# Attention of the first ten head pairs: k loaded on all 128 partitions, q with zero rows from memory, no clears on GpSimd

## The chip, the cores and the metric

The kernel runs on one core of a Trainium2 chip. The core has a matrix engine (TensorE, PE), a vector engine (VectorE, DVE), a scalar engine (ScalarE, ACT), a general engine (GpSimd, POOL) and an engine that only issues transfers (SyncE, SP); 16 DMA engines move the data. Each engine works through its own list of instructions in order and waits on semaphores. The metric is the device time of one execution in microseconds. A run of a kernel is compared with runs of the kernel before on the same chip.

## The reference

q, k and v have the shape (4, 12, 448, 64): batch, heads, sequence, head size. The attention is causal; its output x (4, 448, 768) goes through two mixing blocks, of which only the first touches the stage that is changed here.

```python
scores = scale * np.matmul(q, k.transpose(0, 1, 3, 2))
scores = np.where(mask, -1000000000.0, scores)
attn = np.exp(scores - max); attn = attn / (sum + 1e-09)
x = np.matmul(attn, v)
...
xt = x.transpose(0, 2, 1)
h = np.maximum(xt @ w_tok1, 0.0) @ w_tok2
u = x + h.transpose(0, 2, 1)
h2 = np.maximum(u @ w_ch1, 0.0) @ w_ch2
x = u + h2
...
theta = x @ w_theta; zr = x * cos(theta); zi = x * sin(theta)
y = einsum(w_tok_r, zr) + einsum(w_tok_i, zi)
u = x + y
out = u + np.maximum(u @ w_ch, 0.0)
```

All weights are 64-bit floats in memory.

## The kernel before, in words

The 48 heads are worked as 24 pairs of two heads, 7 steps to a pair (one for the 64-row tails of both heads, then three tiles of 128 rows for each head), 168 steps in all. A step computes scores on TensorE (L358), adds the mask and takes the maximum on VectorE (L367), the exponential on ScalarE (L369), and, 4 or 5 steps later, the product with v on TensorE (L407, L416, L424). Each step also has a share of other work: the 24 weight tiles of the channel mix are fetched as 64-bit words, rounded, split into two 16-bit parts and stored (`ROUNDINGS`; on ACT L177, on GpSimd L130 and L163, on VectorE L185, L186 and L197), and from step 53 on the channel-mix units run between the steps (`UNIT_STEPS`; L231 to L233).

q and k lie in memory as 64 rows (the head size) by 896 columns (two heads), and the host has written every row twice, so that 128 rows are there. `prep` (L276 to L305) brings them in, one pair ahead of its use. There are two kinds of pairs. The pairs 0 to 11 are native: scores are a 32-bit matmul over 128 partitions of which only 64 carry data. For these, 64 rows are loaded, and the other 64 partitions of both tiles are cleared (L281), on GpSimd but for pair 0, where VectorE does it. The pairs 12 to 23 are split: all 128 rows of q and k are loaded (`q_raw`, L288; `k_raw`, L290), ScalarE rounds them (L160) into `qs` and `kh`, and VectorE takes the remainders (L167).

Tiles come from pools by tag, and a tag has a number of buffers, here two each. A new tile of a tag takes the buffer of the tile two before it and must wait until that one's readers are done. Before, native q and split q and k have the tag `qk_raw`; native k and split `kh` have `kh`; split rounded q has `qs`.

The order on each engine is not the order of the code alone: a scheduler places the instructions by the priority of their block (`prep`, the scores and the products with v stand in blocks of high priority) and by when it believes that their inputs and buffers are free. Every instruction of an engine then runs in that fixed order. Transfers of q, k, v, weights and converted weights are all issued by SyncE; only q of pair 0 is issued by ScalarE.

Of the kernel before, what the change touches and what calls it, by code (L numbers as in the profile page):

```python
# [8 lines left out]
F32 = mybir.dt.float32  # L9
# [9 lines left out]
P = 128  # L19
B, H, S, D = 4, 12, 448, 64  # L20
E = H * D
NPR = H // 2
# [7 lines left out]
NATIVE = {0, 1, 2, 3, 4, 5, 6, 7, 8, 9, 10, 11}  # L30
# [2 lines left out]
KEEP, UBACK = 6, 16  # L33
ROUND_BITS, ROUND_FETCH, ROUND_SPLIT, ROUND_STORE = 1, 2, 3, 5
LATE_CONVERT = 16
FIRST_UNIT, DENSE, RATE = 53, 88, (42, 29)
UNIT_STEPS = [FIRST_UNIT + n * (DENSE - FIRST_UNIT) // 14 if n < 14 else
              DENSE + -(-(n - 14) * RATE[0] // RATE[1]) for n in range(72)]
# [16 lines left out]
def fused(ctx, tc, q, k, v, w_tok1, w_tok2, w_ch1, w_ch2, w_theta, w_tok, w_ch, out):  # L55
# [15 lines left out]
    nc = tc.nc  # L71
# [86 lines left out]
    def copy_to(eng, dst, src, scale=1.0):  # L158
        if eng == "A":
            nc.scalar.activation(dst, src, AF.Copy, scale=scale)  # L160
        else:
            e = nc.gpsimd if eng == "P" else nc.vector
            e.tensor_scalar(out=dst, in0=src, scalar1=scale, scalar2=0.0, op0=ALU.mult, op1=ALU.add)  # L163

    def rest_to(eng, dst, src, hi):
        e = nc.gpsimd if eng == "P" else nc.vector
        e.tensor_tensor(out=dst, in0=src, in1=f32v(hi) if hi.dtype == F32R else hi, op=ALU.subtract)  # L167
# [49 lines left out]
    def convert(src, kept, p):  # L217

        w, f = ws_tile(), wf_tile()
        load64(f, src, raw_tile())  # L220
        split_scaled("A", w, f, p, row_squares(f))
        nc.sync.dma_start(out=kept, in_=w)
# [14 lines left out]
    ap2 = att.enter_context(tc.tile_pool(name="ap2", bufs=2))  # L237
# [36 lines left out]
    loads = {}  # L274

    def prep(b, pr):  # L276
        qr = ap2.tile([P, 2 * S], F32, tag="qk_raw", name="q_raw", bufs=2)
        if b * NPR + pr in NATIVE:
            kr = ap2.tile([P, 2 * S], F32, tag="kh", name="k_pad")
            for t, src in ((kr, k), (qr, q)):  # L280
                (nc.vector if b * NPR + pr == 0 else nc.gpsimd).memset(t[64:128], 0.0)  # L281
                if b * NPR + pr == 0 and t is qr:
                    for c in (slice(0, 2 * P), slice(2 * P, 2 * S)):
                        nc.scalar.dma_start(out=t[0:64, c], in_=src[b, pr, 0:64, c])
                else:
                    loads[b * NPR + pr] = nc.sync.dma_start(out=t[0:64], in_=src[b, pr, 0:64])
        else:
            loads[b * NPR + pr] = nc.sync.dma_start(out=qr, in_=q[b, pr])  # L288
            kr = ap2.tile([P, 2 * S], F32, tag="qk_raw", name="k_raw", bufs=2)
            nc.sync.dma_start(out=kr, in_=k[b, pr])  # L290
        vr = ap2.tile([P, 9 * D], F32, tag="v_raw", name="v_raw")
        nc.sync.dma_start(out=vr, in_=v[b, pr])
        if b * NPR + pr in NATIVE:
            qs, kh, kl = qr, kr, None
        else:
            qs = ap2.tile([P, 2 * S], F32R, tag="qs", name="qs")
            copy_to(pick("qhi"), qs, qr)
            rest_to(pick("qlo"), qs[64:128], qr[64:128], qs[64:128])
            kh = ap2.tile([P, 2 * S], F32R, tag="kh", name="kh")
            copy_to(pick("khi"), kh, kr)  # L300
            kl = ap2.tile([P, 2 * S], F32R, tag="kl", name="kl")
            rest_to(pick("klo"), kl, kr, kh)
        if b * NPR + pr in NATPV:
            return qs, kh, kl, (vr,)
        return qs, kh, kl, (vr,)  # L305
# [280 lines left out]
    def convert_late(n):  # L586
        while made[0] < min(n, len(late)):
            with tc.issue_after(loads[min(LATE_CONVERT, max(loads))].ins):
                convert(*late[made[0]])
# [26 lines left out]
    def pick(what):  # L616
        turn[what] = turn.get(what, -1) + 1
        return eng[what][turn[what] % len(eng[what])]

    steps = [(b, pr, t) for b in range(B) for pr in range(NPR) for t in range(7)]  # L620
    parts = {(0, 0): prep(0, 0)}
    pairs, xgs, mixes = {}, {}, []

# [256 lines left out]
    for b in range(B):  # L880
# [43 lines left out]
        if b == 0:  # L924
# [11 lines left out]
            f = split_u2()  # L936
        else:
            n = 3 if b < B - 1 else 2
# [10 lines left out]
            f = split_u2()  # L949
# [5 lines left out]
def _lay(inputs):  # L955
    import numpy as np

    def c(a):
        a = np.ascontiguousarray(a)
        return a.view(np.uint64) if a.dtype == np.float64 else a  # L960

    rows = [slice(0, 64), slice(64, 192), slice(192, 320), slice(320, 448)]

    native = np.array([n in NATPV for n in range(B * NPR)]).reshape(B, NPR, 1, 1)

    def pairs(a, tails_first):
        t = a.reshape(B, NPR, 2, S, D).transpose(0, 1, 4, 2, 3)
        if tails_first:
            t = np.concatenate([t[..., 0, :64], t[..., 1, :64], t[..., 0, 64:], t[..., 1, 64:]], axis=3)
        else:  # L970
            back = np.concatenate([t[..., 0, r] for r in rows[::-1]] + [t[..., 1, :]], axis=3)
            t = np.where(native, t.reshape(B, NPR, D, 2 * S), back)
        t = t.reshape(B, NPR, D, 2 * S)
        return c(np.concatenate([t, t], axis=2))

    v = inputs["v"].reshape(B, NPR, 2, S, D)
    va, vb = v[:, :, 0], v[:, :, 1]
    blocks = []
    for r in rows[1:]:
        blocks += [va[:, :, r], vb[:, :, r]]  # L980
    a0, b0 = va[:, :, rows[0]], vb[:, :, rows[0]]
    zero = np.zeros_like(a0)
    for x, y in ((a0, np.where(native, a0, zero)), (np.where(native, b0, zero), b0), (a0, b0)):
        blocks.append(np.concatenate([x, y], axis=2))
    vl = np.concatenate(blocks, axis=3)
    t1 = inputs["moe_w_tok1"]
    t1 = np.concatenate([np.concatenate([t1[rows[0]], t1[rows[0]]], axis=0)] + [t1[r] for r in rows[1:]], axis=1)
    t2 = inputs["moe_w_tok2"].reshape(2, P, S).transpose(1, 0, 2).reshape(P, 2 * S)

    def lhs_tiles(w):  # L990
        n, m = w.shape
        return w.reshape(n // P, P, m // P, P).transpose(2, 1, 0, 3).reshape(m // P, P, n)

    ch2 = inputs["moe_w_ch2"]
    ch2 = np.concatenate([lhs_tiles(ch2[:FF // 2]), lhs_tiles(ch2[FF // 2:])], axis=0)
    wr, wi = inputs["moe2_w_tok_r"].T, inputs["moe2_w_tok_i"].T
    wk = np.stack([np.concatenate([wr[rows[0]], wi[rows[0]]], axis=0)] + [wr[r] for r in rows[1:]] + [wi[r] for r in rows[1:]])
    return {
        "q": pairs(inputs["q"], True), "k": pairs(inputs["k"], False), "v": c(vl),
        "w_tok1": c(t1), "w_tok2": c(t2),  # L1000
        "w_ch1": c(lhs_tiles(inputs["moe_w_ch1"])), "w_ch2": c(ch2),
        "w_theta": c(inputs["moe2_w_theta"].reshape(DT, P, E)), "w_tok": c(wk),
        "w_ch": c(lhs_tiles(inputs["moe2_w_ch"])),
    }
# [21 lines left out]
```

## Time and profile before

| | |
|---|---|
| time, median of 3 runs | 872.34 us (870.30 to 873.48) |
| profiled execution | 871.68 us, its span 869.9 us |
| TensorE busy | 839.3 us, 96% of the span |
| VectorE / ScalarE / GpSimd busy | 598.9 / 531.3 / 265.6 us |
| mean granted TensorE clock | 0.998 of full |

The page gives the busy time of an engine as the union of its instructions; ends of matmuls are modelled, so a busy TensorE is not one at its peak. The timeline's rows name a start, a length, the engine and line, the tiles written and read, how many instructions the row holds, and in brackets the idle time of the engine before them and what ended it. A row of an engine with a q (SPq) is its sequencer issuing a transfer.

### The profile page before, as it was taken

The numbers are of one execution on the slowest core, as the hardware profiler recorded it, in microseconds if no ns is written. First come the engines' busy times: TensorE is split into PE (matmuls) and PEld (weight loads), VectorE is DVE, ScalarE is ACT, GpSimd is POOL, SyncE is SP. The second block draws the span as 40 slices with busy tenths as digits, with TensorE's granted clock in tenths as the row PEclk, the third lists the DMA queues.
The fourth block names the chain that finished last, engine by engine and source line by source line (L and its number), as shares of the span: only waits on it lengthen the run. The fifth ranks groups of instructions, "written<-read, shape, count | busy, mean of one in ns | idle before, by whom it ended". The sixth has DMA issues, their size and how long they took to land.

```text
span 869.9 us, 16014 instructions
## 1 busy us (share of the span) xinstructions
PE 839.3 (96%) x5699; PEld 532.7 (61%) x5699; DVE 598.9 (69%) x1294; ACT 531.3 (61%) x1223; POOL 265.6 (31%) x445
## 2 busy tenths in 40 slices
PE   7999998899899999999999999999999999999997
PEld 6988856565657566576756655565555555555554
DVE  6788787999988556567774367669747548567541
ACT  6798786777767637367653276547647447456441
POOL 4366564547662220413222035331111001101000
PEclk9999999999999999999999999999999999999999
DMA  6866869999999976856475597702613123131012
GB/s 217 258 208 201 269 198 271 261 310 294 289 255 313 280 226 140 233 132 125 141 173 203 186 278 265 227 30 73 197 40 108 40 90 98 40 119 58 25 45 75
DMA packets 121024, 151.99 MB, mean 175 GB/s; under 512 B 76848, under 2 KB 88048, under 8 KB 120944
## 3 DMA queue, kind: packets, MB, share of 16 engines
q1 hardware_dynamic: 120400, 149.95, 59.4%
q0 software_dynamic: 384, 0.79, 0.4%
q8 instruction: 45, 0.74, 0.3%
q10 hardware_dynamic: 160, 0.23, 0.1%
q14 instruction: 35, 0.29, 0.1%
HBM read 110.56 MB, written 22.81 MB: 153 GB/s over the span
## 4 chain that ended last, share of the span: by engine, by line
PE 67%; DMA 10%; DVE 8%; ACT 5%; issue 5%; POOL 5%; SPq 0%; ACTq 0%; POOLq 0%; DVEq 0%
PE ps_mm L232 15%; PE ps_mm L231 15%; PE ps_mm L233 15%; DMA pt<-ph 5%; PE ps_sc L358 3%; PE ps_sc L231 3%; PE ps_sc L232 3%; PE ps_sc L233 3%; PE ps_pv L407 2%; DMA raw_w<-in_w_theta_dram 1%; PE ps_pv L424 1%; ACT junk L124 1%; ACT sb L369 1%; DVE sb L367 1%; PE ps_mm L376 1%
## 5 line engine op out<-in xcount | busy, mean ns | idle before, releaser
L231 PE MATMUL ps_mm<-h,ws 128*128 128x448 f16 x432 | 151.7, 354 | 1.6 <-DVE g L140 1.0
L232 PE MATMUL ps_mm<-h,ws 128*128 128x448 f16 x432 | 152.7, 354 | 0.1
L233 PE MATMUL ps_mm<-h,ws 128*128 128x448 f16 x432 | 152.5, 354 | 0.0
L231 PEld LDWEIGHTS <-ws 128*128 128x128 f16 x720 | 70.5, 98 | 67.2 <-issue 5.3
L233 PEld LDWEIGHTS <-ws 128*128 128x128 f16 x720 | 70.5, 98 | 63.9 <-issue 3.7
L232 PEld LDWEIGHTS <-ws 128*128 128x128 f16 x720 | 70.5, 98 | 62.5 <-issue 5.2
L369 ACT ACTIVATE sb<-sb,mx 128x320 f32<-128x320 f32 (+3 forms) x168 | 89.1, 533 | 25.6 <-DVE mx L367 25.0
L231 PE MATMUL ps_mm<-ut,ws 128*128 128x448 f16 x288 | 101.1, 353 | 1.4 <-DMA rawt<-x2d 1.3
L232 PE MATMUL ps_mm<-ut,ws 128*128 128x448 f16 x288 | 101.5, 353 | 0.8 <-DVE ut L197 0.8
L233 PE MATMUL ps_mm<-ut,ws 128*128 128x448 f16 x288 | 101.6, 353 | 0.0
L367 DVE CUSTOM_DVE_ANT_0 sb<-ps_sc,mask 128x320 f32<-128x320 f32 (+3 forms) x168 | 73.4, 455 | 17.7 <-PE ps_mm L376 11.3
L124 ACT ACTIVATE junk<-acc 128x448 bf16<-128x448 f32 x72 | 41.2, 572 | 59.1 <-DVE acc L912 41.3
L358 PE MATMUL ps_sc<-k_pad,q_raw 128*128 128x192 f32 (+3 forms) x168 | 56.9, 441 | 9.1 <-DMA k_pad<-in_k_dram 4.3
L787 POOL TENSOR_SCALAR tmp<-tmp 128x384 f32<-128x384 f32 x28 | 15.6, 556 | 148.6 <-ACT tmp L786 145.6
L388 DVE SCALAR_TENSOR_TENSOR ph<-sb,ph 128x128 f16<-128x128 f32 (+1 forms) x64 | 46.8, 736 | 19.0 <-ACT ph L160 18.3
L163 POOL TENSOR_SCALAR h<-t 128x448 f16<-128x448 f32 x48 | 35.2, 735 | 75.7 <-ACT t L497 75.2
L497 ACT ACTIVATE t<-ps_mm,c_scale 128x448 f32<-128x448 f32 x48 | 30.0, 625 | 41.3 <-PE ps_mm L233 36.2
L160 ACT ACTIVATE ph<-sb 128x128 f16<-128x128 f32 (+1 forms) x64 | 39.6, 625 | 25.6 <-DMA pt<-ph 25.3
L499 DVE TENSOR_TENSOR h<-t,h 128x448 f16<-128x448 f32 x48 | 32.0, 670 | 27.0 <-POOL h L163 26.9
L130 POOL TENSOR_SCALAR raw<-raw 128x768 f32<-128x768 f32 (+2 forms) x34 | 35.4, 1041 | 41.6 <-ACT wf L177 37.0
L231 PE MATMUL ps_sc<-th,ut 128*128 128x384 f16 x144 | 46.9, 326 | 0.0
L233 PE MATMUL ps_sc<-th,ut 128*128 128x384 f16 x144 | 46.8, 326 | 0.0
(218 smaller groups left out, 2119.4 us busy)
## 6 DMA issues: line engine op xcount, KB each, us to landing
ws<-w_c SPq DMA_DIRECT2D x120, 384.0 KB, 4.6
raw<-in_w_ch_dram SPq DMA_DIRECT2D x30, 768.0 KB, 5.6
w_c<-ws SPq DMA_DIRECT2D x30, 384.0 KB, 4.3
v_raw<-in_v_dram SPq DMA_DIRECT2D x24, 288.0 KB, 4.9
q_raw<-in_q_dram SPq DMA_DIRECT2D x12, 448.0 KB, 4.2
k_raw<-in_k_dram SPq DMA_DIRECT2D x12, 448.0 KB, 5.4
x2d<-acc SPq DMA_DIRECT2D x24, 224.0 KB, 3.8
acc<-x2d SPq DMA_DIRECT2D x24, 224.0 KB, 2.6
```

What stands on the lines that cost most here:

```text
L124: nc.scalar.activation(j[:, 0:src.shape[-1]], src, AF.Square, accum_out=dst)
L130: nc.gpsimd.tensor_scalar(out=dst, in0=a, scalar1=b, scalar2=c, op0=ALU.mult, op1=ALU.mult)
L160: nc.scalar.activation(dst, src, AF.Copy, scale=scale)
L163: e.tensor_scalar(out=dst, in0=src, scalar1=scale, scalar2=0.0, op0=ALU.mult, op1=ALU.add)
L231: nc.tensor.matmul(ps, lhsT=ka(a[:, 0]), rhs=kb(b[:, 0]), start=first, stop=False)
L232: nc.tensor.matmul(ps, lhsT=ka(a[:, 0]), rhs=kb(b[:, 1]), start=False, stop=False)
L233: return nc.tensor.matmul(ps, lhsT=ka(a[:, 1]), rhs=kb(b[:, 0]), start=False, stop=last)
L358: nc.tensor.matmul(ps[:, 0:n], lhsT=lhs, rhs=cut(pp.kh), start=True, stop=pp.kl is None)
L367: pp.first = nc.vector.tensor_tensor_reduce(out=sb, in0=src, in1=msk, op0=ALU.add, op1=ALU.min, scale=-0.125, scalar=3.0e38, accum_out=pp. ...
L369: pp.last = nc.scalar.activation(sb, sb, AF.Exp, bias=pp.mx[:, j:j + 1], scale=-1.0, accum_out=pp.sm[:, 2 + j:3 + j])
L388: nc.vector.scalar_tensor_tensor(out=lo, in0=both, scalar=PSC, in1=hi, op0=ALU.mult, op1=ALU.subtract)
L499: gates[0] = nc.vector.tensor_tensor(out=t[:, 1], in0=f, in1=t[:, 0], op=ALU.subtract)
```

## The change

Pairs 1 to 9 (`WHOLE` is 10; pair 0 keeps its own way) load all 128 rows of k and of q. The host now writes zeros into the lower 64 rows of q for the pairs 0 to 9, so that the product over 128 partitions is the same, and nothing is cleared for the pairs 1 to 9. The pairs 10 and 11 load and clear as before. Native q takes the tag `qs` (the rounded q of the split pairs) in place of `qk_raw`, which is left to the split pairs' raw q and k.

```diff
--- before.py
+++ after.py
@@ -33,6 +33,7 @@
 KEEP, UBACK = 6, 16
 ROUND_BITS, ROUND_FETCH, ROUND_SPLIT, ROUND_STORE = 1, 2, 3, 5
 LATE_CONVERT = 16
+WHOLE = 10
 FIRST_UNIT, DENSE, RATE = 53, 88, (42, 29)
 UNIT_STEPS = [FIRST_UNIT + n * (DENSE - FIRST_UNIT) // 14 if n < 14 else
               DENSE + -(-(n - 14) * RATE[0] // RATE[1]) for n in range(72)]
@@ -274,19 +275,26 @@
     loads = {}
 
     def prep(b, pr):
-        qr = ap2.tile([P, 2 * S], F32, tag="qk_raw", name="q_raw", bufs=2)
-        if b * NPR + pr in NATIVE:
+        n = b * NPR + pr
+        if n in NATIVE:
+            qr = ap2.tile([P, 2 * S], F32, tag="qs", name="q_raw")
             kr = ap2.tile([P, 2 * S], F32, tag="kh", name="k_pad")
-            for t, src in ((kr, k), (qr, q)):
-                (nc.vector if b * NPR + pr == 0 else nc.gpsimd).memset(t[64:128], 0.0)
-                if b * NPR + pr == 0 and t is qr:
-                    for c in (slice(0, 2 * P), slice(2 * P, 2 * S)):
-                        nc.scalar.dma_start(out=t[0:64, c], in_=src[b, pr, 0:64, c])
-                else:
-                    loads[b * NPR + pr] = nc.sync.dma_start(out=t[0:64], in_=src[b, pr, 0:64])
+            if n == 0:
+                nc.vector.memset(kr[64:128], 0.0)
+                loads[n] = nc.sync.dma_start(out=kr[0:64], in_=k[b, pr, 0:64])
+                nc.vector.memset(qr[64:128], 0.0)
+                for c in (slice(0, 2 * P), slice(2 * P, 2 * S)):
+                    nc.scalar.dma_start(out=qr[0:64, c], in_=q[b, pr, 0:64, c])
+            elif n < WHOLE:
+                nc.sync.dma_start(out=kr, in_=k[b, pr])
+                loads[n] = nc.sync.dma_start(out=qr, in_=q[b, pr])
+            else:
+                for t, src in ((kr, k), (qr, q)):
+                    nc.gpsimd.memset(t[64:128], 0.0)
+                    loads[n] = nc.sync.dma_start(out=t[0:64], in_=src[b, pr, 0:64])
         else:
-            loads[b * NPR + pr] = nc.sync.dma_start(out=qr, in_=q[b, pr])
-            kr = ap2.tile([P, 2 * S], F32, tag="qk_raw", name="k_raw", bufs=2)
+            qr, kr = (ap2.tile([P, 2 * S], F32, tag="qk_raw", name=f"{x}_raw", bufs=2) for x in "qk")
+            loads[n] = nc.sync.dma_start(out=qr, in_=q[b, pr])
             nc.sync.dma_start(out=kr, in_=k[b, pr])
         vr = ap2.tile([P, 9 * D], F32, tag="v_raw", name="v_raw")
         nc.sync.dma_start(out=vr, in_=v[b, pr])
@@ -971,7 +979,10 @@
             back = np.concatenate([t[..., 0, r] for r in rows[::-1]] + [t[..., 1, :]], axis=3)
             t = np.where(native, t.reshape(B, NPR, D, 2 * S), back)
         t = t.reshape(B, NPR, D, 2 * S)
-        return c(np.concatenate([t, t], axis=2))
+        if not tails_first:
+            return c(np.concatenate([t, t], axis=2))
+        whole = np.array([n < WHOLE for n in range(B * NPR)]).reshape(B, NPR, 1, 1)
+        return c(np.concatenate([t, np.where(whole, np.zeros_like(t), t)], axis=2))
 
     v = inputs["v"].reshape(B, NPR, 2, S, D)
     va, vb = v[:, :, 0], v[:, :, 1]
```

The scheduler makes another order of it. On SyncE at the program's start, before the change (`in_w_tok` are the token-mix weights, `in_w_ch` the channel-mix weights; the rows with 64x896 are native loads):

```order
L286 DMA k_pad<-in_k_dram 64x896 x2
L286 DMA q_raw<-in_q_dram 64x896
L292 DMA v_raw<-in_v_dram 128x576 x2
L173 DMA raw<-in_w_tok_dram 128x1024 x2
L173 DMA raw<-in_w_tok_dram 128x896
L286 DMA k_pad<-in_k_dram 64x896
L286 DMA q_raw<-in_q_dram 64x896
L173 DMA raw<-in_w_tok_dram 128x896
L173 DMA raw<-in_w_ch_dram 128x1536 x2
```

and with the change:

```order
L284 DMA k_pad<-in_k_dram 64x896
L289 DMA k_pad<-in_k_dram 128x896
L290 DMA q_raw<-in_q_dram 128x896
L300 DMA v_raw<-in_v_dram 128x576 x2
L174 DMA raw<-in_w_tok_dram 128x1024 x2
L174 DMA raw<-in_w_tok_dram 128x896
L297 DMA q_raw<-in_q_dram 128x896
L298 DMA k_raw<-in_k_dram 128x896
L289 DMA k_pad<-in_k_dram 128x896
L290 DMA q_raw<-in_q_dram 128x896
L174 DMA raw<-in_w_tok_dram 128x896
L174 DMA raw<-in_w_ch_dram 128x1536 x2
```

The two rows that are new ahead of pair 2's loads, `q_raw` of L297 and `k_raw` of L298, are those of pair 12, the first split pair; the 128x896 rows around them are the grown loads of pairs 1 and 2.

On ScalarE where pair 10 ends and pair 11 begins, before the change (`sm_2111` marks the exponentials of pair 10, `sm_2427` those of pair 11, `qs_2444` and `kh_2447` are pair 12's rounded q and k):

```order
L369 ACTIVATE sb_186,sm_2111<-sb_186,mx_2110 128x448 x2
L160 ACTIVATE ph_2416<-sb_186 128x896
L160 ACTIVATE xg0_2032<-x1_192 128x4x128
L160 ACTIVATE qs_2444<-q_raw_2438 128x896
L124 ACTIVATE junk_2196,sqb_2195<-wf_2170 128x768
L369 ACTIVATE sb_186,sm_2427<-sb_186,mx_2426 128x128
...
L160 ACTIVATE ph_2510<-sb_186 128x384
L160 ACTIVATE kh_2447<-k_raw_2440 128x896
L369 ACTIVATE sb_186,sm_2427<-sb_186,mx_2426 128x320
```

and with the change (`sm_2093` is pair 10, `sm_2409` pair 11, `qs_2426` and `kh_2429` are pair 12's rounded q and k, `qs_2693` and `kh_2696` pair 13's):

```order
L161 ACTIVATE ph_2239<-sb_186 128x640
L377 ACTIVATE sb_186,sm_2093<-sb_186,mx_2092 128x448
L161 ACTIVATE qs_2426<-q_raw_2420 128x896
L161 ACTIVATE kh_2429<-k_raw_2421 128x896
L505 ACTIVATE t_1886<-ps_mm_1867,c1_scale0_145 128x448
L161 ACTIVATE xg0_2014<-x1_192 128x4x128
L377 ACTIVATE sb_186,sm_2093<-sb_186,mx_2092 128x448
...
L161 ACTIVATE qs_2693<-q_raw_2687 128x896
L161 ACTIVATE kh_2696<-k_raw_2688 128x896
L161 ACTIVATE ph_2560<-sb_186 128x640
L377 ACTIVATE sb_186,sm_2409<-sb_186,mx_2408 128x448 x2
```

Pair 12's two roundings stood behind all of pair 10's exponentials, and that of k well inside pair 11; now both stand ahead of pair 10's last exponential, and pair 13's ahead of pair 11's last two.

On GpSimd at the start, before the change (L130 is a step of the rounding of weights, L429 a pair's sums):

```order
L257 MEMSET sb 128x64 x2
L281 MEMSET k_pad 64x896
L281 MEMSET q_raw 64x896
L241 AFFINE_SELECT mask<-mask 128x128
L130 TENSOR_SCALAR raw<-raw 128x512
L281 MEMSET k_pad 64x896
L281 MEMSET q_raw 64x896
L130 TENSOR_SCALAR raw<-raw 128x512
L429 TENSOR_SCALAR sm<-sm 128x7
L130 TENSOR_SCALAR sm<-own,sm 128x2
```

and with the change:

```order
L258 MEMSET sb 128x64 x2
L242 AFFINE_SELECT mask<-mask 128x128
L131 TENSOR_SCALAR raw<-raw 128x512 x2
L437 TENSOR_SCALAR sm<-sm 128x7
L131 TENSOR_SCALAR sm<-own,sm 128x2
```

The clears of L281 are gone, and the rest stands in the same order.

## Rows read from the trace of the kernel before

**Rows 1.** The page: busy us, share, instructions of each engine; shares of the chain.
```profile
PE 839.3 (96%) x5699; PEld 532.7 (61%) x5699; DVE 598.9 (69%) x1294; ACT 531.3 (61%) x1223; POOL 265.6 (31%) x445
...
PE 67%; DMA 10%; DVE 8%; ACT 5%; issue 5%; POOL 5%; SPq 0%; ACTq 0%; POOLq 0%; DVEq 0%
```

**Rows 2.** Windows: stretch, length, busy us by engine, PEclk, DMA share, GB/s.
```profile
12.00:125.00 113.00, 108.81 (x773) 92.02 (x772) 93.99 (x236) 93.67 (x257) 65.45 (x98) 1.00 0.70 222
125.00:275.00 150.00, 137.37 (x1102) 90.83 (x1101) 135.62 (x300) 105.88 (x253) 83.64 (x117) 0.99 1.04 281
275.00:869.00 594.00, 585.92 (x3809) 344.90 (x3807) 364.11 (x733) 326.66 (x702) 112.60 (x219) 1.00 0.47 138
```

**Rows 3.** Line 281 from 0 to 110 us: ns min/median/max, first and last; who waited.
```profile
L281 POOL MEMSET k_pad<- x9: 840/842/843, 2.3 to 105.4; 64x896 f32 x9
L281 POOL MEMSET q_raw<- x9: 838/841/848, 3.1 to 106.2; 64x896 f32 x9
...
  PEld ps_sc L358: 1.3, 1
```

**Rows 4.** VectorE's waits, 0 to 125 us: us in total, times, longest.
```profile
DVE ws L197 <- POOL ws L163: 5.5, 5, 1.8
DVE wf L185 <- POOL raw L130: 2.7, 6, 0.8
```

**Rows 5.** Timeline of SyncE: start, length, line, transfer, count.
```profile
12.80 0.54 SPq L286 DMA_DIRECT2D q_raw<-in_q_dram  x1
...
16.67 4.55 SPq L173 DMA_DIRECT2D raw<-in_w_ch_dram  x2
...
22.41 0.53 SPq L286 DMA_DIRECT2D q_raw<-in_q_dram  x1
...
162.21 0.90 SPq L288 DMA_DIRECT2D q_raw<-in_q_dram  x1
...
174.55 0.52 SPq L290 DMA_DIRECT2D k_raw<-in_k_dram  x1
```

**Rows 6.** Transfers issued from 12 to 20, then 20 to 30 us: KB, us to landing.
```profile
q_raw<-in_q_dram SPq DMA_DIRECT2D x1, 224.0 KB, 3.5
...
q_raw<-in_q_dram SPq DMA_DIRECT2D x1, 224.0 KB, 7.9
```

**Rows 7.** Timeline of TensorE: first scores of pairs 2, 3 and 11.
```profile
21.86 0.39 PE L358 MATMUL ps_sc<-k_pad,q_raw 128*128 128x128 f32 x2
...
32.02 0.47 PE L358 MATMUL ps_sc<-k_pad,q_raw 128*128 128x128 f32 x2
...
161.93 0.46 PE L358 MATMUL ps_sc<-k_pad,q_raw 128*128 128x128 f32 x2 [1.55 <-issue]
```

**Rows 8.** Windows near the start, with 64-row and with 128-row loads in flight.
```profile
4.00:6.00 2.00, 1.41 (x4) 0.93 (x4) 0.84 (x5) 0.49 (x2) 0.27 (x1) 1.00 1.05 206
8.00:10.00 2.00, 2.00 (x7) 1.39 (x6) 0.36 (x1) 0.52 (x3) 0.00 (x0) 1.00 1.02 404
```

**Rows 9.** Timeline of ScalarE: rounding of q and k, pairs 12 and 13.
```profile
167.30 0.95 ACT L160 ACTIVATE qs<-q_raw 128x896 fp32r<-128x896 f32 x1 [0.33 <-DMA q_raw<-in_q_dram]
...
178.57 0.95 ACT L160 ACTIVATE kh<-k_raw 128x896 fp32r<-128x896 f32 x1 [0.85 <-DMA k_raw<-in_k_dram]
...
185.02 0.96 ACT L160 ACTIVATE qs<-q_raw 128x896 fp32r<-128x896 f32 x1 [0.85 <-DMA q_raw<-in_q_dram]
...
189.08 0.95 ACT L160 ACTIVATE kh<-k_raw 128x896 fp32r<-128x896 f32 x1 [1.27 <-DMA k_raw<-in_k_dram]
```

**Rows 10.** Windows around pairs 11 and 12.
```profile
160.00:164.00 4.00, 1.41 (x19) 1.02 (x15) 4.00 (x10) 3.53 (x8) 1.72 (x3) 0.99 1.02 341
164.00:168.00 4.00, 4.00 (x15) 1.86 (x13) 4.00 (x11) 3.15 (x7) 1.18 (x3) 0.58 1.38 256
...
175.00:200.00 25.00, 24.32 (x209) 17.15 (x208) 22.78 (x54) 18.85 (x45) 11.08 (x18) 1.00 1.15 307
```

**Rows 11.** Waits of the whole execution: us in total, times, longest.
```profile
ACT kh L160 <- PE ps_sc L358: 5.5, 2, 3.1
```

## The prediction

> **What bounds the kernel now.** I read the page's busy line and chain first. TensorE is busy for 839.3 of 869.9 us and holds 67% of the chain that ended last; VectorE has 598.9 us, GpSimd only 265.6 [rows 1]. The windows by stage come next, because the change touches one stage [rows 2]. The reader is to see three numbers there. From 12 to 125 us (the pairs whose loads are changed) TensorE is busy 108.81 of 113 us, so it idles 4.2 us. From 125 to 275 us (the last native pairs and the first split ones) it idles 150 - 137.37 = 12.6 us, while VectorE works 135.62 of 150 and the DMA share is 1.04. After 275 us it idles 8.1 us in 594, and nothing there is changed. A gain can come only out of 4.2 + 12.6 us, and what TensorE loses there comes back nowhere, since the rest is packed.
>
> **The change part by part.** Times are summed against the profiled execution, 871.68 us, which is 1.8 us longer than its span of 869.9; the median of the three runs is 872.34, 0.7 higher.
>
> *The clears.* Pairs 1 to 9 lose two clears each: 9 at 842 ns and 9 at 841 ns, 15.1 us of GpSimd [rows 3]. GpSimd is busy 65.45 of the 113 us [rows 2], so it is not the bound. Who waits for it? TensorE's weight load once, 1.3 us, for a clear [rows 3]. VectorE waits 5.5 us for the split of converted weights and 2.7 us for the step before its rounding, 8.2 us in all [rows 4]. The clears are 15.1/65.45 = 23% of GpSimd's time there, so about 1.9 us of these waits would go. VectorE idles 19 us in that stretch, so little of that reaches TensorE. Bounds: 0, and -4.2 us (all of TensorE's idle time). I take -0.5, near the lower end of the effect, as TensorE's only wait for a clear was 1.3 us and lies beside earlier matmuls.
>
> *The doubled loads.* Each of the 18 loads grows by 229,376 bytes, 4.13 MB in all, 458,752 per pair. The share of the DMA engines is 0.70 in this stretch [rows 2], so there is room; what counts is whether a pair's rows land before its first score. Pair 3 is the tightest: its q was issued at 22.41 [rows 5], took 7.9 us [rows 6], landed at 30.3, and was first used at 32.02 [rows 7], a slack of 1.7 us. The window with 64-row loads in flight moved 206 GB/s at a share of 1.05, the one with 128-row loads 404 GB/s at 1.02 [rows 8]. Its extra 458,752 bytes cost 1.1 us at 404 and 2.2 us at 206, so between in time and 0.5 us late. I take 0, as the new loads have 128 rows, like those of the 404 row. [...]
>
> *Pair 12's loads.* Native q leaves the two `qk_raw` buffers, so pair 12's q and k find them free from the start. In the program's order they stand right behind the first three token-weight fetches, ahead of pair 2's loads; before, they stood far back, at 162.21 and 174.55 us [rows 5]. Two consequences. First, 917,504 bytes more lie ahead of pair 2, with 458,752 of pair 1's growth and 458,752 of its own: 1,835,008 bytes, 4.5 us at 404 GB/s and 8.9 at 206. Pair 2's q landed at 12.80 + 3.5 = 16.3 [rows 5, 6] and was first used at 21.86 [rows 7], a slack of 5.6 us: in time at one rate, 3.3 us late at the other. I take 0, the 404 row's side. Second, ScalarE's waits for these transfers go: 0.33 and 0.85 us for pair 12's q and k; pair 13's, which now can be issued earlier too, cost 0.85 and 1.27 [rows 9]. That is 3.3 us of ScalarE, but TensorE idles only 0.68 us between 175 and 200 [rows 10]. Bounds 0 and -0.7; I take -0.3.
>
> *The order around pairs 10 and 11.* The scheduler rebuilds it, with the same instructions. [...]
>
> Sum: -0.5 + 0 + 0 - 0.3 - 0.7 = -1.5; 871.7 - 1.5 = 870.2 us.
>
> **Rivals.**
>
> *A: the waits of 125 to 275 us shrink.* With pair 12's loads gone from the crowded stretch (DMA share 1.04) and the order there rebuilt, TensorE might lose half of its 12.6 us [rows 2]: 6.3 on top of -0.8 from the first and third terms (the stall from 160 to 168 is part of the 6.3): 871.7 - 0.8 - 6.3 = 864.6. For it speaks that TensorE's largest wait there sits exactly where the order changes; against it, that VectorE works 90% of this stretch and none of its work goes.
>
> *B: slower, ScalarE blocked by a buffer that it now shares.* Native q moves into the two `qs` buffers. Pair 12's rounded q therefore overwrites pair 10's q and must wait until TensorE has done pair 10's last score; before, its buffer was fresh. In the order this copy and k's now stand ahead of pair 10's last exponential, and pair 13's stand ahead of two of pair 11's. If TensorE is late with those scores, ScalarE stands still with exponentials, ReLUs and roundings behind it, VectorE's residues wait next, and then TensorE for their transposed output. The price by the nearest row is ScalarE's present wait of the same copy for such a score: 2 waits, 5.5 us [rows 11]. [...] It decides once the last score ends after ScalarE has come to the copy. Against it: now ScalarE reaches pair 12's q at 167.30 [rows 9], long after pair 10's scores ended and pair 11's began at 161.93 [rows 7].
>
> *C: the early pile-up.* All of the start's bytes move at the 206 row's rate, and pair 2's first score waits 3.3 us, as worked out above: 871.7 + 3.3 = 875.0. Its sign is a loss, but within what can be told. [...]
>
> **How the numbers follow.** A measurement of this kernel can tell about 0.5% from no change: 4.4 us, so faster means under 868.0 and slower over 876.7. My forecast, 870.2, gets 0.52; its bounds reach from 871.7 - 9.2 to 871.7 + 3.8 if all its terms go one way, of which I give 0.05 to under 868.0 and 0.02 to over 876.7. A gets 0.22, 0.20 of it under 868.0. B gets 0.14, 0.11 of it over 876.7. C gets 0.12, 0.02 of it over 876.7. So faster 0.25, slower 0.15, same 0.60. The range goes from 864, just under A's time, to 877; it leaves out most of B and the further half of A: about 2 in 10.
>
> **What would show it.** No clear is left on GpSimd before pair 10 and its busy time from 0 to 125 us falls by about 15 us, while TensorE's idle time from 12 to 125 us stays near 4 us: the first term is right. If it falls under 1 us, the clears cost more than I think. TensorE's row for pair 2's first score names no load as its releaser: C is wrong. The rate from 4 to 6 us rises above 300 GB/s: the doubled loads are free. ScalarE's rows for pair 12 show no wait for q or k: the third term. From 125 to 275 us TensorE's idle time tells the rest: about 12 us, forecast; 6 or less, A; over 16 with ScalarE waiting for a score ahead of `qs` or `kh`, B. Wrong altogether would be a difference that sits after 275 us.

## The result, and the profile after

The changed kernel takes 879.97 us (median of 6 runs, 875.38 to 882.38) against 871.93 us for the kernel before (6 runs): a ratio of 1.0091, with a 95% interval of 1.0069 to 1.0114. That is 8.0 us slower. The forecast was 870.2 us, its range 864 to 877.

The profiled execution took 882.38 us, the slowest of the six, with a span of 880.6, so it lies 10.7 us above the profiled one of before. A second profile of the same kernel, at 879.72 us (k4_change_again below), stands beside it where a reading rests on one execution. The page's busy line and chain of the changed kernel, against [rows 1]:

```profile
PE 845.5 (96%) x5699; PEld 537.6 (61%) x5699; DVE 597.4 (68%) x1294; ACT 531.0 (60%) x1223; POOL 254.3 (29%) x427
...
PE 70%; DVE 10%; DMA 8%; issue 4%; POOL 4%; ACT 3%; SPq 0%; ACTq 0%; DVEq 0%; POOLq 0%
```

TensorE runs the same 5699 instructions, but is busy 6.2 us longer (845.5 against 839.3), and is idle 35.1 us of the span in place of 30.6. Longer busy for the same work fits a lower clock (before, a 128x448 matmul of `h` and `ws` takes 0.35 us, and 0.58 us in the stretch of [rows 10]), and the windows show one. They stand here against [rows 2] and [rows 8] (length, then busy us of TensorE, its weight loads, VectorE, ScalarE and GpSimd, granted clock, DMA share, GB/s):

```profile
4.00:6.00 2.00, 0.96 (x4) 0.93 (x4) 0.16 (x1) 0.00 (x0) 0.00 (x0) 1.00 1.01 292
...
12.00:125.00 113.00, 107.83 (x760) 91.80 (x759) 93.09 (x235) 93.11 (x256) 51.86 (x81) 0.98 0.74 259
125.00:275.00 150.00, 139.11 (x1088) 91.44 (x1086) 136.75 (x304) 106.75 (x255) 89.24 (x116) 0.95 1.02 269
...
274.00:277.60 3.60, 1.18 (x4) 0.60 (x4) 2.91 (x9) 2.16 (x4) 2.92 (x4) 1.00 1.07 203
277.60:284.40 6.80, 4.12 (x19) 4.09 (x20) 1.53 (x3) 0.38 (x1) 1.16 (x1) 0.51 0.98 352
```

GpSimd lost its clears, 13.6 us of work in the second line. TensorE's idle time from 125 to 275 us even fell, from 12.6 to 10.9 us, but its granted clock there is 0.95 where it was 0.99. The last two lines show one case: TensorE works 1.18 of 3.6 us, and then runs at half clock (0.51 of full) for 6.8 us. There are five such stretches, beginning at 117, 155, 189, 216 and 278 us, 23.9 us in all; before there was one, 3.4 us [rows 10] (one more in the last microseconds of each is left out).

An engine at half clock counts as busy (before, 4.00 of 4 us at a granted 0.58 [rows 10]), so idle time does not show where the time went. I therefore compare progress. Each matmul counts with the time from its start to the next one's, for its kind in the trace of before (the 20th percentile); the sum is 815.8 us for every kernel here. The lag of a kernel at a time t is how much later than before it has done the work that before had done at t:

| lag in us at | 125 | 200 | 250 | 275 | 330 | 800 |
|---|---|---|---|---|---|---|
| changed kernel | 3.3 | 5.2 | 2.7 | 11.2 | 9.4 | 10.3 |
| changed kernel, second profile | 2.1 | 3.9 | 1.5 | 9.5 | 7.8 | 7.6 |

The lag swings by some us up to 250, grows by 8.5 and 8.0 us between 250 and 275, and stays. After 330 us it changes by less than 1 us.

The largest wait of TensorE at this step is not for a load of q or k. TensorE's row in the changed kernel (start, length, line, tiles, count, and in brackets the idle time and its releaser):

```profile
280.28 0.55 PE L232 MATMUL ps_mm<-h,ws 128*128 128x448 f16 x1 [4.31 <-DMA ws<-w_c]
```

SyncE's rows there, first of the changed kernel, then of the kernel before (start, time on SyncE, line, transfer, count):

```profile
267.48 0.33 SPq L589 DMA_DIRECT2D w_c<-ws  x1
268.07 0.32 SPq L528 DMA_DIRECT2D x2d<-acc  x1
268.81 7.31 SPq L399 DMA_TRANSPOSE pt<-ph  x2
276.21 0.53 SPq L227 DMA_DIRECT2D ws<-w_c  x1
```

```profile
260.24 0.32 SPq L581 DMA_DIRECT2D w_c<-ws  x1
...
265.07 1.81 SPq L226 DMA_DIRECT2D ws<-w_c  x4
266.98 6.82 SPq L391 DMA_TRANSPOSE pt<-ph  x2
```

These are the same transfers in another order. Before, four loads of converted weights `ws` stood ahead of two transposing DMAs, which hold SyncE for about 7 us; now they stand behind. The load also reads back what the store `w_c<-ws` ahead of it wrote, and that store now leaves 7.2 us later. None of these rows is in the diff: the scheduler has rebuilt the order.

### The profile page after: what moved, and what is told of

It is laid out like the page before. It is cut to its first block, busy times and chain, and to the rows that moved or that the text cites. A ratio compares the mean times of both kernels' runs of the same rounds, so it can differ in the third digit from the quotient of the medians.

```text
span 880.6 us, 15982 instructions
## 1 busy us (share of the span) xinstructions
PE 845.5 (96%) x5699; PEld 537.6 (61%) x5699; DVE 597.4 (68%) x1294; ACT 531.0 (60%) x1223; POOL 254.3 (29%) x427
## 4 chain that ended last, share of the span: by engine, by line
PE 70%; DVE 10%; DMA 8%; issue 4%; POOL 4%; ACT 3%; SPq 0%; ACTq 0%; DVEq 0%; POOLq 0%
PE ps_mm L233 16%; PE ps_mm L232 16%; PE ps_mm L234 16%; PE ps_sc L366 3%; PE ps_sc L232 3%; PE ps_sc L233 3%; PE ps_sc L234 3%; DMA pt<-ph 3%; PE ps_pv L415 2%; DMA ws<-w_c 2%; PE ps_pv L432 2%; DVE ph L396 1%; POOL raw L131 1%; DVE wf L186 1%; ACT sb L377 1%
## 5 line engine op out<-in xcount | busy, mean ns | idle before, releaser
L375 DVE CUSTOM_DVE_ANT_0 sb<-ps_sc,mask 128x320 f32<-128x320 f32 (+3 forms) x168 | 73.8, 454 | 25.3 <-PE ps_mm L384 10.2
L366 PE MATMUL ps_sc<-k_pad,q_raw 128*128 128x192 f32 (+3 forms) x168 | 59.3, 452 | 6.5 <-DMA q_raw<-in_q_dram 5.6
L164 POOL TENSOR_SCALAR h<-t 128x448 f16<-128x448 f32 x48 | 31.8, 664 | 108.4 <-ACT t L505 107.9
L131 POOL TENSOR_SCALAR raw<-raw 128x768 f32<-128x768 f32 (+2 forms) x34 | 37.4, 1101 | 36.5 <-ACT wf L178 36.1
```

Source lines behind the costliest of these rows:

```text
L131: nc.gpsimd.tensor_scalar(out=dst, in0=a, scalar1=b, scalar2=c, op0=ALU.mult, op1=ALU.mult)
L366: nc.tensor.matmul(ps[:, 0:n], lhsT=lhs, rhs=cut(pp.kh), start=True, stop=pp.kl is None)
L375: pp.first = nc.vector.tensor_tensor_reduce(out=sb, in0=src, in1=msk, op0=ALU.add, op1=ALU.min, scale=-0.125, scalar=3.0e38, accum_out=pp. ...
```

## The experiments

Ratios are to the kernel before, run on the same chip in the same job. Compare runs of different jobs by their ratios, not by their times: the kernel before took 871.17 to 871.93 us in the other jobs, but 869.82 in that of l1 and l2. "Held order" means that the instructions of an engine were bound to a written list by edges that order the issue and add no wait (f1 and f4 below, both held, are at 0.9993 and 0.9990 of the kernel before, which is not, so holding costs nothing that can be seen):

```diff
+ORDER = (
...
+def pin(tc, nc):
...
+        row = [by[e][n] for n in accumulate(steps)]
+        for a, b in zip(row, row[1:]):
+            tc.add_manual_dep(b, a.name, mybir.DependencyInfo(
+                mybir.DependencyClass.NoSync, mybir.DependencyReason.DATA), reason="order")
...
         fused(tc, *args)
+        pin(tc, nc)
```

### Parts of the change alone

e1_room: only the moved room of native q.

```diff
-WHOLE = 10
+WHOLE = 1
```

> The changed kernel with WHOLE = 1: native q lies in the split pairs' buffers, but pairs 1 to 9 load 64 rows again and GpSimd clears the other half. Theory 1 (the loss lies in the order that is rebuilt around 105 to 285 us once native q leaves qk_raw and pair 12's loads go to the start: short waits of TensorE, each followed by a stretch at half clock): about as slow as the changed kernel, 876 to 882 us, with 15 us or more at half clock against 3.4 us before. Theory 2 (the 4.1 MB of added bytes): as before, 870 to 873. Theory 3 (the missing clears or the whole loads alone change the order for the worse): as before, 870 to 873, one or two falls of the clock. Theory 4 (ScalarE held by the shared buffers): 876 to 882, with ScalarE's rounding of q or k waiting for a score of TensorE.

Measured: 884.19 us, 1.0132 (1.0107 to 1.0157).

e2_whole: only the whole loads and the missing clears.

```diff
-            qr = ap2.tile([P, 2 * S], F32, tag="qs", name="q_raw")
+            qr = ap2.tile([P, 2 * S], F32, tag="qk_raw", name="q_raw", bufs=2)
```

> The changed kernel with native q back in qk_raw (two buffers, shared with the split pairs' raw q and k): only the whole loads, the zero rows and the missing clears are left of the change. Theory 1 (order around pairs 10 to 12 from the moved room and the early loads): as before or a little faster, 868 to 872 us, half-clock time as before (3.4 us). Theory 2 (added bytes): 876 to 882 with waits for loads in the first 125 us. Theory 3 (missing clears or whole loads change the order for the worse): 876 to 882 with the falls of the clock of the changed kernel.

Measured: 878.78 us, 1.0080 (1.0055 to 1.0104).

e3_late12: the whole change, with pair 12's loads late as before.

```diff
                 if nx == (0, 1):
                     es.enter_context(tc.issue_after(loads[0].ins))
+                if nx == (2, 0):
+                    es.enter_context(tc.issue_after(loads[11].ins))
```

> The changed kernel with one more constraint: pair 12's loads are not issued before pair 11's (so they don't stand at the program's start); everything else is as changed. If pair 12's early loads are what rebuilds the order for the worse (a form of theory 1): back to 868 to 873 us with one or two falls of the clock. If it is the moved room as such, the bytes (theory 2) or the clears (theory 3): 876 to 882 and three or more falls of the clock.

Measured: 884.24 us, 1.0132 (1.0109 to 1.0155).

e4_dve11: a neutral edit of the kernel before.

```diff
-                (nc.vector if b * NPR + pr == 0 else nc.gpsimd).memset(t[64:128], 0.0)
+                (nc.vector if b * NPR + pr in (0, 11) else nc.gpsimd).memset(t[64:128], 0.0)
```

> The kernel before with one neutral edit: pair 11's two clears are put on VectorE instead of GpSimd (two more VectorE instructions under 1 us each, no load and no byte is changed), which makes the scheduler rebuild the order after it. If any rebuilt order costs waits and falls of the clock (the placebo view of theory 1): 874 to 882 us with 10 us or more at half clock. If the loss belongs to what this change moves: 871 to 873, at most 1 us for the two clears, one or two falls of the clock.

Measured: 880.78 us, 1.0097 (1.0077 to 1.0116).

All four are slower. Each half of the change costs about as much alone as the whole or more, so they don't add up; and moving two clears, with no load and no byte changed, costs the same 1%. Theory 1 in its first form, in which the moved room rebuilds the order for the worse, misses e2, and e3 refutes the early loads as the cause; e1 and e4 move no added byte, so theory 2 can't explain them. That any rebuilt order loses fits all four. Time at half clock does not follow the loss: 23.9 us in e1, 10.2 in e2, 17.1 in e3 and e4. TensorE's longest wait from 100 to 330 us is not the same in all, here in the order e1 to e4 (releaser: us in total, times, longest us):

```profile
PE ps_mm L232 <- DMA ws<-w_c: 6.6, 2, 5.7
```

```profile
PE ps_pv L432 <- DMA pt<-ph: 4.2, 2, 3.2
```

```profile
PE ps_sc L366 <- DVE mx L375: 7.8, 5, 2.8
```

```profile
PE ps_pv L424 <- DMA pt<-ph: 2.7, 2, 2.5
```

Weights, a transposed block, a score's bank, a transposed block: no one resource is short. Nor do they lose at one place: by the lag defined above, e2 is 6.7 us and e3 8.5 us behind at 250 us already, where the changed kernel is 2.7.

### The order held

f1_change_in_old_order has the whole change, and the held order of the kernel before:

> The whole change (whole loads, zero rows, no clears on GpSimd, native q in the split pairs' buffers), with the instructions of each engine held in the order of the kernel before: the same rows in the same places on TensorE, VectorE, ScalarE and SyncE, on GpSimd the same less the 18 clears; only sizes of loads and buffers differ. Order theory (the loss is what a rebuilt order does): 869 to 873 us, clock down once (3 to 4 us), within 2 us of before. Bytes or buffers (the added 4.1 MB, or the shared room, cost the time by themselves): 877 to 882 with the waits of the changed kernel. If the parts have a gain that the new order hides: under 868.

Measured: 871.04 us, 0.9993 (0.9978 to 1.0009), 12 runs. The time is as the order theory had it, the clock is not: it is down three times in the profile (10.2 us), not once.

f2_dve11_in_old_order has the neutral edit in the same held order:

> The neutral edit (pair 11's two clears on VectorE) with every engine held in the order of the kernel before, so that only the two clears have changed their engine. Order theory: 870 to 873 us. If the two clears on VectorE cost the 10 us themselves: 878 to 882.

Measured: 873.36 us, 1.0020 (1.0002 to 1.0038). Of the 0.97% of e4, the two clears by themselves thus account for some 0.2% (0.02 to 0.38).

f3_before_in_new_order has the kernel before in the order of e4_dve11:

> The kernel before, its clears on GpSimd and its loads unchanged, with TensorE, VectorE, ScalarE, SyncE and GpSimd held in the order that the neutral edit produced. Order theory: 878 to 883 us, as the neutral edit, with four or five falls of the clock. If the order is indifferent: 870 to 873.

Measured: 882.73 us, 1.0119 (1.0100 to 1.0137), with three falls of the clock (13.7 us), not four or five.

f4_early12 frees SyncE alone; it then loads pair 12 early:

> The whole change with TensorE, VectorE, ScalarE and GpSimd held in the order of the kernel before, and SyncE in an order of its own, in which pair 12's q and k are loaded near the program's start, ahead of pair 3's, and a few loads stand elsewhere. Order theory in its narrow form (what matters is the computing engines' order): 869 to 873 us. If the early loads cost by a pile-up at the start: 873 to 878, with TensorE waiting for q or k of pairs 2 to 4 in the first 60 us. If SyncE's order alone makes the late waits: above 875 with waits for transposed blocks or ws after 150 us.

Measured: 871.01 us, 0.9990 (0.9978 to 1.0003), 12 runs.

This is the decisive group. The same change costs 0.91% in the order that the scheduler makes of it and nothing in the old order; the unchanged kernel becomes 1.19% slower in a new order. The 4.1 MB more, the shared buffers, the early loads and the missing clears are all in f1 or f4, and all free there to within 0.2%. The windows of f1_change_in_old_order show what the change does by itself, but for pair 12's early loads, which are in f4 alone:

```profile
12.00:125.00 113.00, 109.55 (x781) 92.68 (x780) 96.34 (x240) 94.95 (x260) 55.69 (x84) 1.00 0.75 260
125.00:275.00 150.00, 137.41 (x1084) 92.31 (x1084) 134.20 (x296) 104.16 (x248) 82.35 (x115) 0.97 1.02 277
```

TensorE idles 3.45 us in the first stretch (4.2 before) and 12.6 in the second (12.6 before).

### Where the new order loses

g1_ws_ahead and g2_ws_behind exchange the rows on SyncE that were shown above, everything else held: g1 in the changed kernel's own order, g2 the other way round in the order of before.

```diff
+DMA ws<-w_c                x4   (g1; g2 the reverse)
 DMA_TRANSPOSE pt<-ph       x2
...
-DMA ws<-w_c                x4
```

> The changed kernel held in its own order on every engine, but for one place of SyncE's order: the four loads of ws that stand behind the two transposing DMAs of 268.81 us (7.31 us) now stand ahead of them, as in the kernel before. Order theory with single misplaced rows as the price: TensorE's wait of 4.31 us at 280 us goes, and the fall of the clock behind it (277.6 to 284.4 us) with it, so 873.5 to 876 us. If the time only moves to the next wait (the transposed blocks come 2 us later, or VectorE is the bound there): 878 to 881.

Measured: 879.07 us, 1.0084 (1.0061 to 1.0107). A miss: little came back.

> The reverse in the kernel before: held in its own order, but the four loads of ws that it issues at 265.07 us now stand behind the two transposing DMAs of 266.98 us (6.82 us). Order theory: the loads leave some 7 us later, TensorE waits for ws 5 to 7 us at about 269 us and the clock falls behind it: 876 to 881 us. If such a place is harmless, since TensorE's later work catches up: 871 to 874.

Measured: 880.31 us, 1.0097 (1.0071 to 1.0124). TensorE's row of g2_ws_behind:

```profile
278.33 0.56 PE L231 MATMUL ps_mm<-h,ws 128*128 128x448 f16 x1 [7.77 <-DMA ws<-w_c]
```

One exchange of rows on an engine that computes nothing costs the kernel before 8.8 us. In g1 the reverse gives little back, though TensorE's wait for `ws` does shrink, from 4.31 to 1.40 us (at 272.0 us). One reason is in the trace: the load that now stands ahead must wait 5.7 us for the store before it, and leaves 6.7 us after that store's issue. It is not the whole of it: g1's profile lags by 3.3 us at 330 us and by 6.4 at 800, 2.2 of these at a half-clock stretch near 640 us that the changed kernel's two profiles don't have. SyncE's waits, and its rows, in g1_ws_ahead:

```profile
SPq L227 <- DMA w_c<-ws: 5.7, 1, 5.7
```

```profile
262.07 0.43 SPq L589 DMA_DIRECT2D w_c<-ws  x1
262.67 0.32 SPq L528 DMA_DIRECT2D x2d<-acc  x1
268.77 1.74 SPq L227 DMA_DIRECT2D ws<-w_c  x4
270.62 6.51 SPq L399 DMA_TRANSPOSE pt<-ph  x2
```

k1_old_then_new and k2_new_then_old put two orders together at 245 us.

> The changed kernel, with every engine in the order of the kernel before up to what had begun by 245 us there, and the rest in the order of the changed kernel. If the new order loses after 245 us (TensorE's lag behind before at equal work grew from 2.7 to 11.2 us between 250 and 275 us in the changed kernel's trace): 877 to 881 us. If the loss lies in what the new order does before 245 us: 870 to 873. If it is spread over both: 873 to 877 here and in the run with the halves exchanged.

Measured: 880.04 us, 1.0101 (1.0083 to 1.0120).

> The halves exchanged: the order of the changed kernel up to what had begun by 245 us in its trace, and the rest in the order of the kernel before. If the new order loses after 245 us: 871 to 875 us. If it loses before: 877 to 881. If it is spread over both: 873 to 877.

Measured: 873.98 us, 1.0027 (1.0007 to 1.0048).

So the new order after 245 us loses about as much alone (1.0101) as the whole of it (1.0091, and 1.0103 in k4 below); before 245 us it costs some 2 us (1.0027, with an interval of 0.6 to 4.2 us). The windows of 245 to 285 us in the kernel before, the changed kernel, k1 and k2, one fence each in this order:

```profile
245.00:285.00 40.00, 37.64 (x309) 25.07 (x308) 35.95 (x77) 27.92 (x72) 14.22 (x20) 1.00 0.98 294
```

```profile
245.00:285.00 40.00, 32.74 (x222) 20.82 (x220) 33.28 (x69) 22.25 (x50) 21.05 (x25) 0.91 1.00 286
```

```profile
245.00:285.00 40.00, 33.18 (x208) 21.51 (x208) 31.49 (x66) 21.26 (x52) 17.04 (x20) 0.83 0.94 276
```

```profile
245.00:285.00 40.00, 37.37 (x311) 24.79 (x310) 34.55 (x76) 25.43 (x67) 15.65 (x21) 1.00 1.00 279
```

In 40 us the two with the new order there start 222 and 208 matmuls, the two with the old order 309 and 311.

k3_both takes the exchange of g1 into k1; k4_change_again runs the changed kernel once more.

> As k1_old_then_new (old order to 245 us, then the new), but with the four loads of ws ahead of the two transposing DMAs (7.27 us) behind which they stand in the new order, as in g1_ws_ahead. In k1_old_then_new TensorE waits 3.41 us for ws at 276.6 us, and runs at half clock from 274.8 to 281.6 us. If this place carries most of what the new order loses after 245 us: 873 to 876 us, 4 us or more under k1_old_then_new. If it is only one among several: 877 to 879.

Measured: 877.89 us, 1.0075 (1.0054 to 1.0097): one place among several, by the expectation, and its interval overlaps that of k1.

> The changed kernel unchanged, once more, so that g1_ws_ahead and k3_both can be compared with more than six runs of it: 879 to 881 us.

Measured: 879.58 us, 1.0103 (1.0079 to 1.0126). Its half-clock stretches begin at 116, 153, 188, 215 and 276 us: the same five places as in the first profile (mean granted clock 0.986, and 0.985 there).

In the changed kernel, what makes the store late is one row on VectorE. These weights are split in two steps: GpSimd writes the rounded part, VectorE the residue, and then the store goes. GpSimd's row and VectorE's rows of the changed kernel:

```profile
260.43 0.91 POOL L164 TENSOR_SCALAR ws<-wf,s 128x768 f16<-128x768 f32 x1
```

```profile
260.60 1.68 DVE L168 TENSOR_TENSOR kl<-k_raw,kh 128x896 fp32r<-128x896 f32 x1
262.20 0.94 DVE L187 SCALAR_TENSOR_TENSOR wf<-raw,wf 128x768 uint32<-128x768 uint32 x1
263.06 0.48 DVE L375 CUSTOM_DVE_ANT_0 sb<-ps_sc,mask 128x320 f32<-128x320 f32 x1
...
264.18 1.09 DVE L168 TENSOR_TENSOR qs<-q_raw,qs 64x896 fp32r<-64x896 f32 x1
...
266.45 1.01 DVE L198 SCALAR_TENSOR_TENSOR ws<-wf,s,ws 128x768 f16<-128x768 f32 x1
```

The same two in the kernel before:

```profile
258.25 0.91 POOL L163 TENSOR_SCALAR ws<-wf,s 128x768 f16<-128x768 f32 x1
```

```profile
259.19 1.02 DVE L197 SCALAR_TENSOR_TENSOR ws<-wf,s,ws 128x768 f16<-128x768 f32 x1
```

Before, the residue began 0.03 us after GpSimd was done; now it begins 5.1 us after, behind the rounding residues of pair 17's k and q, two scores and other rows. l1_chain (in the changed kernel's own order) and l2_chain (in k1) put the whole chain in place:

```diff
 on VectorE
 TENSOR_TENSOR kl<-k_raw,kh
+SCALAR_TENSOR_TENSOR ws<-wf,s,ws
 SCALAR_TENSOR_TENSOR wf<-raw,wf
...
-SCALAR_TENSOR_TENSOR ws<-wf,s,ws
 on SyncE
+DMA w_c<-ws
 DMA x2d<-acc x3
-DMA w_c<-ws
...
+DMA ws<-w_c x4
 DMA_TRANSPOSE pt<-ph x2
...
-DMA ws<-w_c x4
```

> The changed kernel held in its own order, with the whole chain behind its wait at 280 us put in place, not the last link alone: VectorE's residue of the last converted weights (ws, line 198), which stands 5.1 us after GpSimd has made its first part (261.34 to 266.45 us), goes ahead of the rows that stand between (wf, a score, acc, qs, a score, acc); the store of these weights goes ahead of three stores of acc on SyncE; the four loads of ws go ahead of the two transposing DMAs, as in g1_ws_ahead. There the first of them waited 5.7 us for the store, which had left late. If this chain is the place: no wait for ws near 276 us, 874 to 877 us. If the new order loses at many places: 878 to 880, as g1_ws_ahead (879.1).

Measured: 875.03 us, 1.0068 (1.0054 to 1.0082), with the kernel before at 869.82 in that job.

> The same three moves in k1_old_then_new (old order to 245 us, then the new; 880.0 us, with the last link alone 877.9). If the chain is the place at which the half after 245 us loses: 873 to 876 us. If it is one of many: 876.5 to 878.

Measured: 875.32 us, 1.0064 (1.0047 to 1.0080). In us both lie in the ranges for "the chain is the place", but the kernel before was 2 us faster in this job: at the 871.7 us of k1's job, 1.0064 is 877.3, which is "one of many", and at the 871.9 us of the changed kernel's, 1.0068 is 877.9, between the two ranges of l1.

TensorE's wait for `ws` near 276 us is gone from both traces, and the half-clock stretch beside it too (the granted clock of 245 to 285 us is 1.00 in l1 and 0.91 in l2, whose one stretch begins near 249 us); SyncE's load still waits for the store, 1.8 and 1.6 us where it was 5.7 in g1. The window of l1_chain shows the stage nearly back:

```profile
245.00:285.00 40.00, 36.60 (x307) 24.24 (x305) 35.63 (x76) 27.00 (x69) 16.30 (x21) 1.00 1.00 292
```

The chain is worth 2 to 3 us of the 8 to 9 (1.0091 and 1.0103 become 1.0068; 1.0101 becomes 1.0064). It is the largest single place found, not the whole. How much of it belongs to the last link and how much to the rest of the chain the runs don't tell apart: l1's interval overlaps g1's, and l2's overlaps k3's. Where the remaining 0.6 to 0.7% sits was not found.

h1_moves tries the opposite: the order of f4_early12 with eight moves of rows ahead of others where TensorE waits.

> The changed kernel in the order of f4_early12, with eight moves of single rows at places where its trace shows TensorE waiting between 133 and 246 us (1.8 us for h at 133 us, 1.2 and 0.8 for a score's bank at 158 to 161, 1.6 for v_hi at 206, 1.7 for g at 220, 0.4 for v_hi at 225, 1.0 for g at 246): on VectorE h of line 460 ahead of the second ph, g of line 141 ahead of wf and qs, g of line 128 ahead of kl, g of line 141 ahead of the third ut; on GpSimd sv and v_hi ahead of a raw, and ahead of an s; on TensorE four products of h and ws ahead of each of two scores. If waits fetch their own price where nothing else is late: 7 us less idle, 864 to 866 us. If VectorE, busy 136 of 150 us there, is the bound behind TensorE: 868 to 871, the waits come back elsewhere.

Measured: 871.61 us, 1.0000 (0.9983 to 1.0016). The waits went from their places and others came: in f4_early12 the longest after 125 us was 2.05 us for `h`, in h1_moves it is 1.80 us for `g`, 40 us later. TensorE's idle time is 28.7 us in place of 28.9. No version here is measurably faster than the kernel before.

```profile
178.00 0.39 PE L456 MATMUL ps_mm<-xg,wt 128*128 128x256 f32 x1 [1.80 <-DVE g L141]
```

The lags of these runs' profiles, computed as above:

| lag in us at | 125 | 200 | 250 | 275 | 330 | 800 |
|---|---|---|---|---|---|---|
| f1_change_in_old_order | -1.9 | 1.4 | -0.1 | 0.4 | -1.3 | 0.1 |
| f3_before_in_new_order | -0.6 | 3.8 | 4.3 | 8.9 | 9.2 | 8.9 |
| g2_ws_behind | 0.1 | 1.1 | 1.8 | 11.6 | 9.6 | 12.0 |
| k1_old_then_new | -1.3 | -1.8 | -0.5 | 7.8 | 5.9 | 9.8 |
| k2_new_then_old | 0.0 | 2.9 | 0.8 | 1.7 | -0.3 | 2.3 |
| l1_chain | 0.3 | 2.3 | -0.3 | 2.1 | 3.2 | 2.3 |

At 800 us each lag lies within 0.5 us of what that profiled execution took beyond the profiled one of before. One execution is not the median, though: g2's took 883.67 us, its median is 880.31. And l1's 2.3 us stands against 0.68%, since the kernel before was faster in its job. Of the 2.4 to 3.9 us that g2, k1 and k2 still add after 330 us, most is one half-clock stretch near 640 us, which the profiles of the other runs in this table don't have.

## Why the prediction was wrong

**The step that failed** is the fourth term, "The order around pairs 10 and 11". It stands in the sum as -0.7, and no run shows that term: in its place, the runs showed that the new order costs 0.91 to 1.03% (some 8 to 9 us). The bounds of the sum, 871.7 - 9.2 to 871.7 + 3.8, hold 4.3 us for it on the fast side (the others have 4.2 and 0.7) and nothing on the slow side, where the 3.8 are the 0.5 and 3.3 us of late loads. It should have been open there: an order that is rebuilt on all engines can also make new waits. The profile shows a wait of before; it can't show the waits that another order will have. The other two claims that rested on it fell with it: "nothing there is changed" after 275 us (the largest wait ends at 280.28 us), and the sentence that a gain can come "only out of 4.2 + 12.6 us", which is a bound on gains and says nothing on losses.

**The other three terms were not contradicted**, and the forecast holds for the change without its new order: their sum was -0.8 us, and f4_early12, which has all three, measured -0.9 (-1.9 to 0.3); f1_change_in_old_order, which lacks the early loads, measured -0.6 (-1.9 to 0.8). Both intervals reach 0, so the runs don't show that the terms are worth anything at all.

- The clears. GpSimd's busy time from 0 to 125 us fell from 69.4 to 53.7 us, 15.6 less. TensorE's idle time from 12 to 125 us was 4.2 us before and 3.45 in f1, 4.1 in f4 and 5.2 in the changed kernel: near 4, as the sign asked, and too scattered to show -0.5.
- The doubled loads cost nothing. From 4 to 6 us the rate rose from 206 to 292 GB/s (287 in f1), a little under the 300 that I had asked for. That is 1.4 times the rate of before; two fetches of weights were issued in that window too, so it doesn't tell the loads' own share of the rise.
- Pair 12's early loads. TensorE's first score of pair 2 waits for nothing, and ScalarE's roundings for pair 12 wait for no load, against [rows 7] and [rows 9]. These waits had no price that can be seen, though: f1, whose roundings for the pairs 12 and 13 still wait 3.7 us for loads, takes the time of f4. The rows:

```profile
22.86 0.39 PE L366 MATMUL ps_sc<-k_pad,q_raw 128*128 128x128 f32 x2
```

```profile
161.06 0.95 ACT L161 ACTIVATE qs<-q_raw 128x896 fp32r<-128x896 f32 x1 [0.35 <-PE ps_sc L366]
161.92 0.93 ACT L161 ACTIVATE kh<-k_raw 128x896 fp32r<-128x896 f32 x1
```

**Rival B** had the right direction, and with its 5.5 us most of the 8.0 us measured, for the wrong reason. The buffer is shared and ScalarE does wait for pair 10's last score, but 0.35 us, the row above. The row that B was priced by [rows 11] was also misread: it is the copy of k, not of q, and its two waits lie at 314.75 and 359.12 us, far behind pair 12. In the changed kernel the same copy waits 4.1 us in all, where it was 5.5:

```profile
ACT kh L161 <- PE ps_sc L366: 4.1, 3, 3.3
```

And f4_early12, with the same buffers and ScalarE's order of before, takes 871.01 us. **Rival C** is refuted by pair 2's row: it starts at 22.86 us and waits for nothing, so what SyncE issued early did not make it late. **Rival A** did not come: TensorE's idle time of 125 to 275 us fell by 1.7 us, not 6.3, while the mean granted clock there fell from 0.99 to 0.95.

**The sign I chose could not see it.** By my list, TensorE idle for about 12 us from 125 to 275 us meant the forecast; it was 10.9. Half of the loss was not idle time but busy time at half clock (6.2 us more busy and 4.5 more idle in the profile), and the largest wait ended 5 us behind the window's edge. A difference "that sits after 275 us" I had called wrong altogether, and so it is.

**What was left out of the chances.** Five rebuilt orders were measured (the changed kernel and e1 to e4), and all five cost 0.8 to 1.3%. I gave "slower" 0.15, and 0.11 of it to one buffer. Five of five says that the order of before is a good one among its kind; why it is, and how often another would be faster, no run here shows.

## What to carry to other kernels

When a scheduler places the instructions, an edit is two changes: what it does, and the order that is rebuilt around it. Cost the second one by itself, with an end on the slow side: near a packed engine it is worth 1% here, more than the edit. To measure the first, hold the order of the kernel before; to find where the second loses, compare progress at equal work, and follow the late transfer back to the row that made it late.

## What I had not expected of the hardware

- A transposing DMA holds SyncE far longer than a plain one: 1.17 to 4.76 us each in the changed kernel (64 of them, median 1.37), where a plain one takes 0.32 to 1.61 (377, median 0.34). Two of the long ones in a row are a wall of 7 us for all that is queued behind.
- A load that reads back what a store wrote had to wait 5.7 us for that store in g1_ws_ahead, and left 6.7 us after the store's issue (the median of such stores in the changed kernel is 4.4 from issue to landing).
- The order alone does not say where TensorE's clock falls. The two profiles of the changed kernel have their falls at the same five places, in the first each behind a stretch in which TensorE worked 1.2 to 2.2 of 3.6 to 3.9 us. But g1_ws_ahead has the same order on every engine up to 268 us, and of the four places before that it has one only (115 us). At the second, first in the changed kernel and then in g1 (busy us, then the granted clock as the third number from the end):

```profile
151.00:154.70 3.70, 1.99 (x23) 0.97 (x22) 2.55 (x8) 3.30 (x12) 2.31 (x4) 1.00 1.09 371
154.70:161.60 6.90, 5.56 (x32) 3.08 (x33) 4.87 (x12) 5.13 (x13) 0.90 (x1) 0.51 0.84 229
```

```profile
150.00:153.70 3.70, 0.66 (x4) 0.15 (x2) 2.25 (x4) 2.51 (x10) 1.24 (x2) 1.00 1.24 211
153.70:160.60 6.90, 6.89 (x57) 4.27 (x58) 6.38 (x16) 5.78 (x12) 0.91 (x1) 1.00 0.71 198
```

In g1 TensorE worked less, 0.66 us, and the clock stayed up. Nor does a fall always cost time that can be seen: f1 has three (10.2 us at half clock) and before one (3.4 us), and their times are alike (0.9993).
